# The per-token bonus factor of units 14 to 23: from TensorE products to GpSimd multiplies and a VectorE sum

## The chip, the cores and the metric

One core of one Trainium2 chip runs the whole kernel. The metric is the device time of one execution in microseconds, the median of several runs; lower is better.

## The reference

Two stages follow one another. The first is a linear attention with decay over 4 batches, 8 heads, 768 tokens and 48 channels per head; the second routes each of the 3072 resulting rows to one of 8 experts.

```python
# attention, for each token t, per batch and head
cur = u*k_t (outer) v_t
y_t = r_t @ (state + cur)
state = w * state + k_t (outer) v_t
# experts, x = y as (3072, 384)
logits = x @ w_gate + modality_bias[modality_id];  e_idx = argmax(logits)
out[mask e] = gate_w[mask e] * (relu(x[mask e] @ w1[e]) @ w2[e])
```

The part of `r_t @ cur` is what the change touches. It equals `d * v_t`, where `d = sum over the 48 channels of r*u*k` is one number per token and head. In the kernel `d` is a tile of 128 tokens by 8 heads.

## The kernel before, in words

**Units.** The attention is cut into 24 units of 128 tokens, `(b, c)` with the chunk `c` (0 to 5) in the outer loop and the batch `b` (0 to 3) in the inner one. A unit's inputs come in two layouts. `turned` (L297) loads r and k with channels on the partitions, as the tile `ud`; `lines` (L306) loads k and v with a token per partition, as the tile `kv`. The input array `in_pt` holds k, r and v side by side for each token; `lines` reads the first and the third.

**One unit on the engines.** GpSimd makes `rc` (r times powers of the decay, `decay`, L318), `kt` (k times powers, for the state, `carry`, L325) and, in `own_keys` (L330), `rk`, the product of `rc` and `kc`. VectorE makes `kc` (k times powers, `keys`, L337) and multiplies the scores by the causal mask (`causal`, tile `at`, L378). TensorE makes the scores (`psc`, L372), then in `values` the state's part of the output (L400), the part from the scores (L407), for chunks 0 to 4 the state's update (`pst`, L418), and last, in `bonus` (L346), the factor `d` of the next unit: eight matmuls with 64 columns of `rk` as weights and two columns of `uw` (w times u, one column per head of a pair) as the moving operand, in fp32. They write columns 384 to 391 of the PSUM tile `pst` in whose first 384 columns the state's update lies; `pst` has one buffer. `taken` (L351) on VectorE copies those columns to `d`, and `own` (L359) on ScalarE multiplies `v` by `d`, head by head, into `dv`. From unit 11 on (`BARE`) VectorE adds `dv` to the output (`token`, L435). From chunk 3 on VectorE adds `pst` to the state (`state`, L469), after ScalarE has decayed it (`fade`, L388).

**What runs beside it.** From step 11 on the same engines also work for the first expert. The rows of a group of two to four units are scored (`logits`, L508; `choose`, L518 to L549), counted and placed (L558 to L580, `ahead`, L704 to L727) and sent to DRAM by indirect DMAs from GpSimd (`send`, L596). Blocks of 128 sent rows come back by DMA (`s_turn`, tiles `mxT` and `mt`), and TensorE multiplies them by the first expert's weights: `s_up` (`phs`, L963), `s_down` (`pos`, L1037 and L1042), with ScalarE and VectorE between them (`hh`, L967; `hl`, L972). Odd steps 11 to 21 hold an `s_up`, the even steps after them the `s_down`.

**Order.** Up to the loop over the remaining blocks (L1380) the order on each engine is written out by hand, in `run`: each engine takes its instructions strictly in that order. In step `i` GpSimd's order is: `own_keys(i+1)`, sends, `decay(i+3)`, the give-out of a finished block (L931 to L933), `carry(i+2)`. SP issues `turned(i+5)`, `lines(i+4)`, then the transposing DMA of the finished unit `i-1` (`flip`, L490), a sixth of the second expert's weights in steps 15 to 20 (`raw`, L871), and the turns. The tags `rk` and `kc` have two buffers, `rc` four, `kv` five.

Of the kernel before, what the change touches and what calls it, by code (L numbers as in the profile page):

```python
# [9 lines left out]
F32 = mybir.dt.float32  # L10
# [6 lines left out]
AX = mybir.AxisListType  # L17

P = 128
B, H, S, D = 4, 8, 768, 48  # L20
NCH = S // P
NPR = H // 2
NT = B * S
DM = H * D
# [14 lines left out]
NJ = 40  # L39

BARE = 11

FILL = {1: 4, 2: 4, 3: 2, 4: 2, 5: 2}

# [9 lines left out]
class _Kernel:  # L54
# [251 lines left out]
    def lines(self, i):  # L306

        b, c = self.units[i]
        kv = self.a.tile([P, 2 * DM], F32, tag="kv", name=f"kv{i}", bufs=5)
        self.nc.sync.dma_start(kv.rearrange("p (q d) -> p q d", q=2), self.pt[b * NCH + c].rearrange("p (q d) -> p q d", q=3)[:, ::2])  # L310
        self.ctx_[i].update(k=kv[:, :DM], v=kv[:, DM:])

    def decay(self, i, n=1):
        nc, u = self.nc, self.ctx_[i]
        u["rc"] = self.a.tile([P, NPR, P], F32, tag="rc", name=f"rc{i}", bufs=4)
        for q in range(n):
            s = slice(q * NPR // n, (q + 1) * NPR // n)
            nc.gpsimd.tensor_mul(u["rc"][:, s], u["rT"][:, s], self.powr[:, s])  # L318
# [7 lines left out]

    def own_keys(self, i):
        nc, u = self.nc, self.ctx_[i]
        u["rk"] = self.a.tile([P, NPR, P], F32, tag="rk", name=f"rk{i}")
        nc.gpsimd.tensor_mul(u["rk"], u["rc"], u["kc"])  # L330

# [16 lines left out]
    def taken(self, i):  # L348
        u = self.ctx_[i]
        u["d"] = self.a.tile([P, H], F32, tag="d", name=f"d{i}", bufs=4)  # L350
        self.nc.vector.tensor_copy(u["d"], u["pd"])  # L351

    def own(self, i, q):
        nc, u = self.nc, self.ctx_[i]
# [35 lines left out]
    def values(self, i):  # L390
        nc, u = self.nc, self.ctx_[i]
        b, c = self.units[i]
        st = self.st[c % 2]
        py = u["py"] = self.ps_y.tile([P, 512], F32, tag="y", name=f"py{i}")
        if c:
            for pr in range(NPR):
                c0 = pr * 2 * D
                for q in range(2):
                    t = slice(64 * q, 64 * q + 64)
                    nc.tensor.matmul(py[t, c0 : c0 + 2 * D], u["rc"][:112, pr, t], st[:112, b, pr, :], start=pr == 0, stop=False, skip_group_check=True)  # L400

        for h in range(H):
            pr, j = divmod(h, 2)
            sl = slice(h * D, (h + 1) * D)
            for q in range(2):
                t = slice(64 * q, 64 * q + 64)
                nc.tensor.matmul(py[t, sl], u["at"][:, j * NPR + pr, t], u["v"][:, sl], start=c == h == 0, stop=h == H - 1 and i >= BARE, skip_group_check=True)  # L407
        if i + 1 < len(self.units):
            pst = u["pst"] = self.ps_s.tile([P, 512], F32, tag="s", name=f"pst{i}")
        if c < NCH - 1:  # L410
            faded = self.early(c)
            for pr in range(NPR if faded else 0):
                c0 = pr * 2 * D
                nc.tensor.matmul(pst[:112, c0 : c0 + 2 * D], self.dg[:112, pr, :], st[:112, b, pr, :], start=pr == 0, stop=False, skip_group_check=True)
            for h in range(H):
                j = h % 2
                sl = slice(h * D, (h + 1) * D)
                nc.tensor.matmul(pst[64 * j : 64 * j + D, sl], u["kt"][:, h, :], u["v"][:, sl], start=not faded, stop=True, skip_group_check=True)  # L418
        if i + 1 < len(self.units):
            self.bonus(i + 1, pst)  # L420

    def owned(self, i):
        nc, u = self.nc, self.ctx_[i]
        py = u["py"]
        if i < BARE:
            for q in range(2):
# [3 lines left out]
    def token(self, i):  # L430
        nc, a, u = self.nc, self.a, self.ctx_[i]
        b, c = self.units[i]
        u["x"] = u["py"][:, :DM]
        if i >= BARE:
            nc.vector.tensor_add(u["x"], u["x"], u["dv"])  # L435
# [17 lines left out]
    def early(self, c):  # L453

        return 0 < c and c * B + B - 1 <= BARE

# [416 lines left out]
    def norm(self, junk, q):  # L873
        self.nc.scalar.activation(junk, self.raw[:, q * WQ : (q + 1) * WQ], AF.Square, accum_out=self.ssq[:, q : q + 1])
# [175 lines left out]
    def run(self):  # L1050
        nc, tc, m = self.nc, self.tc, self.m
# [25 lines left out]
        def plan(step, f):  # L1077
            at.setdefault(step, []).append(f)

        def piece(e, q):  # L1080
            if q == 0:
                self.eid = nc.sync.value_load(self.ctl[:, e : e + 1], min_val=0, max_val=E - 1)
            self.load(self.eid, NQ, q)

        def scales(key, half):
            for _ in self.scales_(key, slice(half, half + 1), self.ps_a, "big"):
                pass
# [13 lines left out]
        plan(3, lambda: fills.append(self.setup4()))  # L1101
        plan(4, lambda: fill(99))
        plan(6, self.setup5)
        O = 2
        first, second = (lambda q: lambda: piece(0, q)), (lambda q: lambda: piece(1, q))
        norm = lambda q: lambda: self.norm(junk, q)
        split = lambda q: lambda: self.split(q)
        for q in range(NQ):
            plan(O + (q + 1) // 2, first(q))
            plan(O + 2 + (q + 1) // 2, norm(q))  # L1110
            plan(15 + q, second(q))
            plan(17 + q, norm(q))
        plan(O + 4, lambda: scales("w1", 0))
        plan(O + 6, lambda: (scales("w2", 1), self.undo()))
        for q, i in enumerate((7, 7, 8, 9, 9, 10)):
# [11 lines left out]
        def each(i, *fs):  # L1127
            for f in fs:
                if live(i):
                    f(i)  # L1130


        def fill(n=1):
            while n and fills:
                g = fills.pop(0)
                if next(g, fills) is not fills:
                    fills.append(g)
                    n -= 1

        for i in range(NU - 1):  # L1140
# [12 lines left out]
            if down is not None:  # L1153
                self.s_high(down, 1)
                self.s_down(down, 0)
            first = i <= BARE
            each(i, self.taken) if i and first else None
# [52 lines left out]
            for p in range(2):  # L1210
                for h in range(2):
                    c, r = divmod(i + 1 - 2 * p - h, B)
# [16 lines left out]
        i, j = NU - 2, NU - 1  # L1229
# [208 lines left out]
```

## Time and profile before

| what | value |
|---|---|
| median of 3 runs | 374.55 us (373.67 to 376.98) |
| the profiled execution's own time | 376.96 us |
| its span | 375.2 us |
| TensorE busy over the span | 340.5 us (91%) |
| VectorE, ScalarE, GpSimd busy | 231.2, 176.7, 165.3 us |
| mean granted TensorE clock | 0.958 |

The profile shows one execution. Its rows of time give the start of a group of instructions, how long the group took, the engine, the line of the kernel, the operation and its tiles, how many instructions there are, and in square brackets how long the engine had been idle before and what ended that. The rows of stretches give for each engine the busy time with the number of instructions, then the granted TensorE clock, the busy share of the DMA engines and the GB/s moved. An fp32 matmul shows as two instructions.

### The profile page before, as it was taken

To read this page: it belongs to the slowest core of one execution; us is meant where nothing else is said; L and a number is where in the kernel's file an instruction comes from. 1 tells how busy PE (TensorE), PEld (TensorE's weight loads), DVE (VectorE), ACT (ScalarE), POOL (GpSimd) and SP (SyncE) were. 2 spreads that over 40 slices of the span, in tenths; PEclk is the share of its full clock that TensorE was granted. 3 is DMA by queue.
4 is the path that set the end of the run, shared out by engine and by line. 5 is a ranking of instruction groups with operands and counts; after the bars stand their busy time and mean duration, and the time that the engine had idled before them with its cause. 6 is when DMAs were issued, how large, how long until landed. Compare 5 with 4: busy or idle time off the path is not lost. (4 is left out here: it accounts for less than half of the span.)

```text
span 375.2 us, 14969 instructions
## 1 busy us (share of the span) xinstructions
PE 340.5 (91%) x5432; PEld 271.4 (72%) x5432; DVE 231.2 (62%) x741; ACT 176.7 (47%) x474; POOL 165.3 (44%) x243
## 2 busy tenths in 40 slices
PE   8976968878999999899999999599899999999883
PEld 3654857766879788687888777387687778887661
DVE  6986737788689969858945863028733322224960
ACT  6557646746646645755764222027222222256720
POOL 7996444395358468554425431014421111202731
PEclk9997869898899999999999999699999999999999
DMA  7997999875779499993546254211752122111110
GB/s 160 257 200 163 271 221 228 160 191 128 142 157 189 114 221 250 210 248 114 166 69 107 86 151 172 63 42 42 271 136 60 42 52 53 42 42 42 42 54 4
DMA packets 61166, 50.31 MB, mean 134 GB/s; under 512 B 47288, under 2 KB 54727, under 8 KB 60864
## 3 DMA queue, kind: packets, MB, share of 16 engines
q1 hardware_dynamic: 57920, 40.21, 50.4%
q0 software_dynamic: 3200, 9.47, 6.9%
q8 instruction: 31, 0.51, 0.6%
q14 instruction: 15, 0.12, 0.1%
HBM read 28.39 MB, written 11.83 MB: 107 GB/s over the span
## 5 line engine op out<-in xcount | busy, mean ns | idle before, releaser
L963 PEld LDWEIGHTS <-whi 128*128 128x128 f16 x1248 | 74.6, 100 | 4.6 <-issue 2.0
L1037 PEld LDWEIGHTS <-hh 128*128 128x128 f16 x416 | 38.9, 98 | 29.8 <-issue 4.2
L359 ACT ACTIVATE dv<-kv,d 128x48 f32<-128x48 f32 x192 | 48.1, 325 | 4.5 <-DVE d L351 4.4
L330 POOL TENSOR_TENSOR rk<-rc,kc 128x512 f32<-128x512 f32 x24 | 30.6, 1274 | 43.9 <-DVE kc L337 16.9
L963 PE MATMUL phb<-mxT,whi 128*128 128x128 f16 x720 | 48.8, 222 | 0.0
L963 PEld LDWEIGHTS <-wlo 128*128 128x128 f16 x624 | 38.0, 98 | 1.5 <-DVE wlo L909 1.5
L318 POOL TENSOR_TENSOR rc<-ud,powr 128x512 f32<-128x512 f32 (+1 forms) x27 | 32.3, 1202 | 12.8 <-PE py L400 7.9
L972 DVE SCALAR_TENSOR_TENSOR hl<-phb,hh 128x256 f16<-128x256 f32 (+1 forms) x45 | 22.7, 512 | 22.4 <-ACT hh L967 18.5
L967 ACT ACTIVATE hh<-phb 128x256 f16<-128x256 f32 (+1 forms) x45 | 20.2, 453 | 34.2 <-PE L963 12.5
L378 DVE TENSOR_TENSOR at<-psc,mask 128x512 f32<-128x512 f32 x48 | 32.3, 683 | 3.4 <-PE psc L372 3.0
L596 POOL DMA_INDIRECT rows<-row,posi x24 | 24.4, 1018 | 21.4 <-issue 15.1
L1042 PEld LDWEIGHTS <-hl 128*128 128x128 f16 x208 | 19.5, 99 | 19.8 <-issue 4.4
L963 PE MATMUL phs<-mxT,whi 128*128 128x128 f16 x480 | 31.4, 224 | 0.0
L372 PE MATMUL psc<-rc,kc 48*64 48x128 f32 x768 | 29.9, 294 | 1.7 <-issue 1.4
L1047 DVE TENSOR_SCALAR fac<-mt,wf 128x1 f32<-128x1 f32 x16 | 3.4, 212 | 44.6 <-ACT otb L923 39.4
L923 ACT ACTIVATE otb<-po,fac 128x384 f32<-128x384 f32 x15 | 8.6, 576 | 47.0 <-PE phb L963 37.1
L1042 PE MATMUL po<-whi,hl 128*128 128x384 f16 x128 | 25.0, 338 | 5.4 <-DVE mt L1337 4.0
L1037 PE MATMUL po<-wlo,hh 128*128 128x384 f16 x128 | 26.3, 326 | 3.0 <-DVE wlo L909 3.0
L407 PE MATMUL py<-kv,at 128*64 128x48 f32 x768 | 27.5, 225 | 1.7 <-DVE row0f L680 1.1
L963 PE MATMUL phb<-mxT,wlo 128*128 128x128 f16 x360 | 27.9, 219 | 1.2 <-DVE wlo L909 1.2
L407 PEld LDWEIGHTS py<-kv,at 128*64 128x64 f32 x768 | 26.5, 142 | 3.2 <-DVE row0f L680 1.8
L909 DVE SCALAR_TENSOR_TENSOR wlo<-raw,ws,whi 128x1024 f16<-128x1024 f32 (+1 forms) x18 | 24.8, 1417 | 5.3 <-ACT whi L904 5.3
(259 smaller groups left out, 654.3 us busy)
## 6 DMA issues: line engine op xcount, KB each, us to landing
ud<-in_pd SPq DMA_DIRECT2D x48, 192.0 KB, 5.0
kv<-in_pt SPq DMA_DIRECT2D x24, 384.0 KB, 5.6
raw<-in_w SPq DMA_DIRECT2D x12, 512.0 KB, 5.6
raw<-in_w SPq DMA_DIRECT2D x2, 1536.0 KB, 6.8
rows<-pad SPq DMA_DIRECT2D x10, 193.0 KB, 2.6
rows<-row,posi POOLq DMA_INDIRECT x24, 4.6
xT<-row SPq DMA_TRANSPOSE x23, 4.2
xn<-rows SPq DMA_TRANSPOSE x16, 3.2
```

Of the source, the lines that this page charges most:

```text
L318: nc.gpsimd.tensor_mul(u["rc"][:, s], u["rT"][:, s], self.powr[:, s])
L330: nc.gpsimd.tensor_mul(u["rk"], u["rc"], u["kc"])
L359: nc.scalar.activation(u["dv"][:, sl], u["v"][:, sl], AF.Copy, scale=u["d"][:, h : h + 1])
L372: nc.tensor.matmul(u["ps"][j][s, pr * P : (pr + 1) * P], u["kc"][r, pr, s], u["rc"][r, pr, :], start=True, stop=True)
L378: nc.vector.tensor_mul(u["at"][:, j * NPR : (j + 1) * NPR, :], u["ps"][j].rearrange("p (q t) -> p q t", q=NPR), self.mask.unsqueeze(1).to_ ...
L407: nc.tensor.matmul(py[t, sl], u["at"][:, j * NPR + pr, t], u["v"][:, sl], start=c == h == 0, stop=h == H - 1 and i >= BARE, skip_group_che ...
L596: i = nc.gpsimd.indirect_dma_start(out=self.rows, out_offset=bass.IndirectOffsetOnAxis(ap=u["posi"][:, b : b + 1], axis=0), in_=u["row"][: ...
L909: self.nc.vector.scalar_tensor_tensor(self.wlo[:, sl], self.raw[:, sl], sc, self.whi[:, sl], ALU.mult, ALU.subtract)
L963: self.nc.tensor.matmul(ph[:, q * P : (q + 1) * P], w[:, c0 : c0 + P], self.xT[:, xq, t * P : (t + 1) * P], start=i == q == 0, stop=i == l ...
L972: self.nc.vector.scalar_tensor_tensor(self.hl[:, f0 : f0 + fb, r], p3, 0.0, self.hh[:, f0 : f0 + fb, r], ALU.max, ALU.subtract)
L1037: self.nc.tensor.matmul(po[:, :DM], self.hh[:, f, t * P : (t + 1) * P], w[:, c0 : c0 + DM], start=n == q == f == 0, stop=False)
L1042: self.nc.tensor.matmul(po[:, :DM], self.hl[:, f, t * P : (t + 1) * P], self.whi[:, c0 : c0 + DM], start=False, stop=f == FB - 1)
```

## The change

A new constant `LATE` is 14. For units 14 to 23:

- `lines` also loads r with a token per partition (tile `r`, four buffers, 128 by 384 fp32), right behind the load of `kv` on SP's queue;
- `own_keys` multiplies r by k and the result by u, two GpSimd instructions of 128 by 384 each, in place of the one of 128 by 512 that made `rk`. The result `ru` takes the buffers of tag `rk`;
- `taken` sums `ru` over the 48 channels of each head on VectorE, in place of the copy out of PSUM;
- `bonus` is not issued, and units 20 to 23, which have no state update, no longer take a `pst` tile.

In step 9 a new `wide_u` loads u, repeated on all 128 partitions, as the tile `ub`.

```diff
+LATE = 14
...
         self.ctx_[i].update(k=kv[:, :DM], v=kv[:, DM:])
+        if i >= LATE:
+            r = self.ctx_[i]["r"] = self.a.tile([P, DM], F32, tag="r", name=f"r{i}", bufs=4)
+            self.nc.sync.dma_start(r, self.pt[b * NCH + c][:, DM : 2 * DM])
+
+    def wide_u(self):
+
+        self.ub = self.c.tile([P, DM], F32, name="ub")
+        self.nc.sync.dma_start(self.ub, self.u.to_broadcast([P, DM]))
...
     def own_keys(self, i):
         nc, u = self.nc, self.ctx_[i]
+        if i >= LATE:
+            t = u["ru"] = self.a.tile([P, NPR * P], F32, tag="rk", name=f"ru{i}")[:, :DM]
+            nc.gpsimd.tensor_mul(t, u["r"], u["k"])
+            nc.gpsimd.tensor_mul(t, t, self.ub)
+            return
...
-        self.nc.vector.tensor_copy(u["d"], u["pd"])
+        if i >= LATE:
+            self.nc.vector.reduce_sum(u["d"], u["ru"].rearrange("p (h d) -> p h d", h=H), axis=AX.X)
+        else:
+            self.nc.vector.tensor_copy(u["d"], u["pd"])
...
-        if i + 1 < len(self.units):
+        if i + 1 < LATE or c < NCH - 1:
             pst = u["pst"] = self.ps_s.tile([P, 512], F32, tag="s", name=f"pst{i}")
...
-        if i + 1 < len(self.units):
+        if i + 1 < LATE:
             self.bonus(i + 1, pst)
...
+        plan(9, self.wide_u)
```

On TensorE, in `values` of unit 14 (`py` is the unit's output, `pst` its state update, `pos` and `hl` belong to the expert's block), before:

```order
L400 MATMUL py_2299<-st_94,rc_1709 64x96 x8
L407 MATMUL py_2299<-kv_1503,at_2080 64x48 x16
L418 MATMUL pst_2324<-kv_1503,kt_91 48x48 x8
L346 MATMUL pst_2324<-uw,rk_2230 64x2 x8
L1042 LDWEIGHTS hl
L1042 MATMUL pos_2233<-whi,hl 128x384
```

and now, with the line numbers of the changed kernel:

```order
L418 MATMUL py_2305<-st_94,rc_1715 64x96 x8
L425 MATMUL py_2305<-kv_1505,at_2091 64x48 x16
L436 MATMUL pst_2330<-kv_1505,kt_91 48x48 x8
L1060 LDWEIGHTS hl
L1060 MATMUL pos_2239<-whi,hl 128x384
```

The eight products for `d` are gone from between the state's update and the next block's product; nothing else has moved. The same holds in the units 13 to 22.

On GpSimd, around the steps 14 and 15, before:

```order
L318 TENSOR_TENSOR rc_2263<-ud_86,powr 128x512
L325 TENSOR_TENSOR kt_89<-kv_1825,wtok 128x384
L330 TENSOR_TENSOR rk_2384<-rc_2055,kc_2266 128x512
L318 TENSOR_TENSOR rc_2435<-ud_87,powr 128x512
L931 TENSOR_TENSOR puts_2438<-ids,none 128x1
```

and now:

```order
L328 TENSOR_TENSOR rc_2269<-ud_86,powr 128x512
L335 TENSOR_TENSOR kt_89<-kv_1831,wtok 128x384
L341 TENSOR_TENSOR ru_2384<-r_1833,kv_1831 128x384
L342 TENSOR_TENSOR ru_2384<-ru_2384,ub 128x384
L328 TENSOR_TENSOR rc_2436<-ud_87,powr 128x512
L949 TENSOR_TENSOR puts_2439<-ids,none 128x1
```

Two multiplies stand where one stood, and they read `r`, `kv` and `ub`, no longer `kc`, which VectorE makes. On VectorE the sum stands where the copy stood, between the same neighbours:

```order
L536 TENSOR_SCALAR xinv_1391<-sx_1390 128x4
L367 TENSOR_REDUCE d_2259<-ru_2009 128x8
L487 TENSOR_TENSOR st_93<-st_93,pst_2127 48x4x48
L539 TENSOR_REDUCE L_2262<-pr_2175 128x32
L487 TENSOR_TENSOR st_93<-st_93,pst_2127 48x4x48
```

Before, the second of these rows was the copy:

```order
L518 TENSOR_SCALAR xinv_1391<-sx_1390 128x4
L351 COPY d_2253<-pst_2116 128x8
L469 TENSOR_TENSOR st_93<-st_93,pst_2116 48x4x48
L521 TENSOR_REDUCE L_2256<-pr_2172 128x32
L469 TENSOR_TENSOR st_93<-st_93,pst_2116 48x4x48
```

Only the operation and its source differ: `ru` in SBUF for `pst` in PSUM.

## The prediction

> **What bounds the kernel now.** I read the busy time by stretch first, cut where the products for `d` that the change removes begin and end, and where the attention's tail ends (columns: length, then TensorE, its weight loads, VectorE, ScalarE, GpSimd busy with counts, granted clock, DMA share, GB/s).
>
> ```profile
> 117.50:191.00 73.50, 72.14 (x1511) 60.92 (x1506) 59.43 (x181) 44.01 (x140) 39.65 (x53) 1.00 0.82 180
> 191.00:235.70 44.70, 44.22 (x587) 34.60 (x585) 26.40 (x140) 13.87 (x33) 16.50 (x42) 1.00 0.47 122
> 235.70:239.70 4.00, 0.01 (x1) 0.04 (x2) 0.46 (x2) 0.00 (x0) 0.00 (x0) 0.80 0.29 49
> ```
>
> In the first stretch TensorE is busy 72.14 of 73.5 us and has no idle that another engine causes: its one stall there, of 1.36 us, is in the next fence. VectorE is busy 59.43 us and leaves 14.07. So TensorE's instruction stream sets the pace, and what is taken out of it moves all that follows. Then I read TensorE's order of time around one of these products (in unit 14's `values`, for unit 15's `d`) and the total of L346 in the stretch.
>
> ```profile
> 126.13 0.53 PE L418 MATMUL pst<-kv,kt 128*48 128x48 f32 x16
> 126.49 0.60 PE L346 MATMUL pst<-uw,rk 112*64 112x2 f32 x16
> 127.02 1.47 PE L1042 MATMUL pos<-whi,hl 128*128 128x384 f16 x8
> 154.40 0.88 PE L372 MATMUL psc<-rc,kc 48*64 48x128 f32 x23 [1.36 <-issue]
> 117.50:191.00 73.50, 5.97 (x160) 5.52 (x160) 1.00 0.82 180
> ```
>
> The last row is L346 alone: 160 instructions, ten units of 16. Not all of the 5.97 us is path, because matmuls overlap: from the start of L346 at 126.49 to the start of the next group at 127.02 it is 0.53 us.
>
> **The change part by part.** *Removed from TensorE:* 10 x 0.53 = 5.3 us, all of it in a stream without gaps, at a granted clock of 1.00. This is the one large term.
>
> *GpSimd:* one multiply of 128x512 becomes two of 128x384.
>
> ```profile
> 117.06 1.04 POOL L325 TENSOR_TENSOR kt<-kv,wtok 128x384 f32<-128x384 f32 x1
> 118.01 1.30 POOL L330 TENSOR_TENSOR rk<-rc,kc 128x512 f32<-128x512 f32 x1
> 119.24 1.30 POOL L318 TENSOR_TENSOR rc<-ud,powr 128x512 f32<-128x512 f32 x1
> 120.47 1.02 POOL L325 TENSOR_TENSOR kt<-kv,wtok 128x384 f32<-128x384 f32 x1
> 124.32 1.28 POOL L330 TENSOR_TENSOR rk<-rc,kc 128x512 f32<-128x512 f32 x1 [2.83 <-DVE ebx L284]
> L330 POOL TENSOR_TENSOR rk<-rc,kc 128x512 f32<-128x512 f32 x10 | 12.8, 1282 | 20.1 <-DVE posi L578 14.4 <-DVE ebx L284 5.7
> L325 POOL TENSOR_TENSOR kt<-kv,wtok 128x384 f32<-128x384 f32 x6 | 6.1, 1019 | 0.0
> ```
>
> `kt` has the new shape, 1.02 us; so 2 x 1.02 - 1.28 = 0.76 us more per unit, 7.6 in all, on an engine that is idle for 73.5 - 39.65 = 33.9 us of the stretch. The row at 120.47 makes the `kt` of unit 16, which TensorE takes two steps later, and `rc` is three units ahead, so 0.76 us is hidden there. What changes more is when it works. Before the `rk` at 124.32 GpSimd idled for 2.83 us until VectorE's `kc` was there (20.1 us ahead of ten `rk`). `ru` needs only `r`, `kv` and `ub`, loaded steps before: GpSimd will run on from `kt` into the two multiplies at once, and no longer leaves VectorE a pause in which to make `kc`.
>
> *VectorE:* the copy becomes a sum, and its small operations meet GpSimd elsewhere.
>
> ```profile
> L351 DVE COPY d<-pst 128x8 f32<-128x8 f32 x12 | 1.9, 157 | 2.5 <-PE pst L346 2.4
> 215.76 0.28 DVE L754 TENSOR_REDUCE en<-pk 128x16 f32<-128x128 f32 x1
> 118.73 2.80 DVE L518 TENSOR_SCALAR xinv<-sx 128x4 int32<-128x4 int32 x1
> 122.69 0.69 DVE L972 SCALAR_TENSOR_TENSOR hl<-phs,hh 128x512 f16<-128x512 f32 x1
> 124.37 0.19 DVE L528 TENSOR_REDUCE mx<-L 128x4 f32<-128x32 f32 x1
> L337 DVE TENSOR_TENSOR kc<-ud,powk x25: 425/684/1823, 6.2 to 178.4; 128x512 f32<-128x512 f32 x23, 128x256 f32<-128x256 f32 x2
> ```
>
> No row has a sum of 384 elements. From 0.19 us for 32 and 0.28 for 128, 0.94 ns per element gives an estimate of 0.52 us; against the copy's 0.16 that is 0.36 more per unit, 3.6 in all. The bounds: 0.12 more (the 0.28 of the 128-element sum) and 1.1 (if a sum is held up by one multiply of 1.02 us as well). I take 0.36: the sum at 124.37 took 0.19 us while `rk` ran from 124.32 to 125.60, so sums are not held up. Other VectorE work is: `xinv`, on 4 elements, took 2.80 us and ended at 121.53, just after `kt` ended at 121.49; and one `kc` took 1823 ns for a median of 684.
>
> How much of this reaches TensorE is read from the distance between a VectorE result and its use. The `hl` that ends at 123.38 is used at 127.02: 3.6 us. The closest pair I found is in steps 16 and 17, where the group's placing also stands:
>
> ```profile
> 142.62 1.91 DVE L723 SCALAR_TENSOR_TENSOR ctl<-done,fur 1x1 int32<-1x1 f32 x1
> 146.19 0.71 DVE L469 TENSOR_TENSOR st<-st,pst 48x192 f32<-48x192 f32 x2
> 148.91 0.53 PE L418 MATMUL pst<-kv,kt 128*48 128x48 f32 x16
> ```
>
> The state's sum ends at 146.90 and frees the only `pst` buffer, which L418 takes at 148.91: 2.0 us. TensorE now comes 0.53 us sooner from the same point, two sums add 0.72, so 0.8 us is left, against perhaps 0.8 more of blocking (0.5 for a placing operation and 0.3 for `kc`, each behind part of a 1.02 us multiply) and less at L723, whose 1.91 us ended with a multiply too. It may just miss there. I book 0.3 us; bounds 0 (all hidden) and 2.6 (both steps late by 1.3). The `d` of the last units comes earlier, since it no longer waits for TensorE, but ScalarE's `dv` is not what TensorE waits for: nothing.
>
> *DMA and SP:* 11 loads of 192 KB more.
>
> ```profile
> ud<-in_pd SPq DMA_DIRECT2D x48, 192.0 KB, 5.0
> 135.00:150.00 15.00, 15.00 (x322) 12.57 (x320) 12.76 (x42) 7.83 (x28) 9.85 (x15) 1.00 1.11 242
> 150.00:165.00 15.00, 13.64 (x266) 11.09 (x263) 12.70 (x36) 10.77 (x34) 7.38 (x10) 1.00 1.18 226
> 51.80 0.78 PE L508 MATMUL pr<-wghl,xT 128*128 128x16 f16 x23 [3.32 <-issue]
> ```
>
> A load of this size lands in 5.0 us and is wanted three steps later, and its buffer is free when it is issued, so on SP it costs only its issue; the flip and the weights' pieces behind it come that much later, with steps to spare. But from 135 to 165 the DMA engines are full, and there about four of these loads come on top. TensorE's stalls "for nothing that the profile shows" fall in such full stretches: 1.36 us at 154.40, 3.32 at 51.80. I take zero, because the program moves only a little against the transfers; bounds -1.36 (the one in the stretch goes) and +3.32 (a second like the longest).
>
> *Sum:* -5.3 + 0.3 = -5.0 us. On the profiled execution: 376.96 - 5.0 = 371.96. Its time lies 2.4 us above the median of the runs, 374.55; on that, **369.55 us**.
>
> **The rivals.** *1. VectorE comes late at the dense places.* `kc` reads two tiles of SBUF, and now meets GpSimd at work in each unit. If it waits for one multiply, 0.36 + 1.02 = 1.38 us per step, 2.76 over steps 16 and 17 against a distance of 2.0 - 0.53 = 1.5: 1.3 us lost, and as much again around steps 18 and 19: 374.55 - 5.3 + 2.6 = 371.85. For it: `xinv` waited 2.80 us through more than one multiply. Against: the second multiply must wait for the first, a break in which VectorE can get in, and other distances are over 3 us. The Trainium skill says so too ("SBUF — State Buffer", Who interferes with whom): VectorE with two SBUF inputs and a GpSimd instruction that reads SBUF exclude each other for the whole instruction, while sums never do on this chip. The rows of `xinv`, `kc` and the sum at 124.37 agree.
>
> *2. VectorE becomes the bound, and the kernel slower.* The place is the whole stretch, the price a wait at `kc` in each unit. It has 14.07 us to spare at the old length; sums take 3.6, so from (14.07 - 3.6) / 10 = 1.05 us of blocking per unit, about one multiply, the stretch is longer than before. At one and a half (1.53 us): 3.6 + 15.3 - 14.07 = +4.8, so 379.4 us. For it: `kc` took 1823 ns once, 1.14 over its median. Against: the 59.43 us already hold blocked time (2.80, 1.91), which moves rather than adds.
>
> *3. One more stall of TensorE's own kind* in the full stretch, by the rows at 154.40 and 51.80 some 1.4 to 3.3 us, say 2.3: 371.85 us again, by another cause.
>
> *4. The gain is absorbed* in the 4 us gap at 235.7.
>
> ```profile
> 207.48 0.22 PE L558 MATMUL pr<-oh,warm 128*128 128x8 f16 x3
> 210.18 0.17 DVE L578 CAST posi<-pos 128x3 int32<-128x3 f32 x1
> 210.62 0.97 POOL L596 DMA_INDIRECT rows<-row,posi  x1 [4.68 <-DVE fur L704]
> SPq L950 <- DMA rows<-row,posi: 4.6, 2, 3.6
> 224.89 9.07 SPq L860 DMA_DIRECT2D rows<-pad  x8
> 235.97 1.26 SPq L950 DMA_TRANSPOSE xn<-rows  x1
> 239.69 2.72 PE L1042 MATMUL po<-whi,hl 128*128 128x384 f16 x8 [4.01 <-DVE mt L1337]
> ```
>
> TensorE waits there for a block that comes through SP: eight pads in a row (9.07 us), then the transposing load. If that chain did not start sooner, the gap would be 9 us and the time 374.55. Against: it begins with sends that wait for positions (210.18), counted by TensorE at 207.48, so it moves with TensorE.
>
> **How the numbers follow.** The forecast 0.52, rival 1 0.18, rival 3 0.15, rival 2 0.08, rival 4 0.07. One per cent, about what a measurement of this kernel can tell from no change, is 3.75 us: faster means below 370.8. Of the forecast 0.49 lies there and 0.03 above; of rivals 1 and 3 0.06 and 0.05; so faster 0.60. Slower, above 378.3, is most of rival 2: 0.06. Same 0.34. The range begins where the saving is whole and the 1.36 us stall goes as well, 374.55 - 5.3 - 1.36 = 367.9, and ends at 373.4: rival 3's upper end, 374.55 - 5.0 + 3.3 = 372.85, and half a microsecond for what rivals 1 and 3 may do together; rivals 2 and 4 lie outside.
>
> **What would show it.** Right: no two-column products after unit 13's; TensorE busy within 1.5 us of the length of the stretch, which is 68 to 69 us from the end of unit 13's state update to the last `d`; sums of 0.4 to 0.6 us; GpSimd's pair right behind `kt`; the gap near 235 still 4 us and 5 us sooner. Wrong: TensorE waiting for `kc`, `st` or `hl` in this stretch, with `kc` over 1 us (rivals 1, 2); new stalls on nothing shown (3); a gap over 6 us (4); or a group after L418 that starts less than 0.5 us sooner than before.

## The result, and the profile after

| kernel | median of its runs | ratio to before, 95% interval |
|---|---|---|
| before (4 runs) | 374.11 us (373.35 to 376.98) | |
| the change (4 runs) | 369.93 us (368.79 to 376.74) | 0.987 (0.982 to 0.992) |

The forecast was 369.55 us, 5.0 below before. By the medians the change took off 4.2 us, by the ratio 4.9. The profiled execution of the change took 370.29 us, with a span of 368.6 us. Some executions of a kernel fall into a slower state, and the ratios here and below leave them out; in the second set of experiments one very low run of the kernel before (368.4 us) puts most of its others into that state, so there I compare the medians of all runs.

The two profiles cannot simply be subtracted: the state's update of unit 13, up to which both kernels give TensorE the same work, begins at 117.17 us before and at 113.31 us after. In nine more profiles of kernels that differ little or not at all ahead of it, it begins between 111.8 and 118.3 us. So I measure from that update's start to the start of the last unit's `values`, which is the same pair of places in every kernel. The stretch before, then of the change (length; TensorE, weight loads, VectorE, ScalarE, GpSimd busy with counts; clock, DMA share, GB/s):

```profile
117.17:194.54 77.37, 76.01 (x1574) 64.17 (x1570) 61.84 (x195) 47.19 (x151) 40.32 (x54) 1.00 0.81 174
```

```profile
113.31:186.39 73.08, 72.07 (x1413) 59.48 (x1409) 64.01 (x194) 46.16 (x150) 46.37 (x63) 1.00 0.89 203
```

TensorE still sets the pace: it is idle for 1.01 us of 73.08. It lost some 160 instructions and 3.94 us of busy time. VectorE gained 2.17 us and GpSimd 6.05. The place around unit 14's state update, and every idle time of TensorE from there to the expert's loop:

```profile
121.84 0.53 PE L436 MATMUL pst<-kv,kt 128*48 128x48 f32 x16
122.30 1.48 PE L1060 MATMUL pos<-whi,hl 128*128 128x384 f16 x8
...
145.50 0.38 PE L981 MATMUL phs<-mxT,whi 128*128 128x128 f16 x4 [0.41 <-issue]
165.85 0.34 PE L1055 MATMUL pos<-wlo,hh 128*128 128x384 f16 x1 [0.55 <-issue]
200.59 0.50 PE L1055 MATMUL pos<-whi,hh 128*128 128x384 f16 x2 [0.26 <-ACT hh L985]
232.47 2.72 PE L1060 MATMUL po<-whi,hl 128*128 128x384 f16 x8 [4.92 <-DVE mt L1356]
```

Before, 0.36 us lay between the start of the state's update and that of the products, and 0.53 between these and `pos`: 0.89 together. Now `pos` follows the update after 0.46. That is **0.43 us saved per unit, not 0.53**. With `L346` gone, the next group does not take its place 0.36 us after the update; it begins 0.10 later. In units 20 to 22, which have no state update, the next group begins 1.02 us after the start of L425 where it was 1.44 after L407: 0.42.

No row in the stretch has TensorE waiting for `kc`, `st` or `hl`. On GpSimd the pair stands right behind `kt`, as forecast:

```profile
116.78 1.01 POOL L335 TENSOR_TENSOR kt<-kv,wtok 128x384 f32<-128x384 f32 x1
117.73 1.00 POOL L341 TENSOR_TENSOR ru<-r,kv 128x384 f32<-128x384 f32 x1
118.82 1.40 POOL L342 TENSOR_TENSOR ru<-ru,ub 128x384 f32<-128x384 f32 x1
121.18 1.28 POOL L328 TENSOR_TENSOR rc<-ud,powr 128x512 f32<-128x512 f32 x1 [0.97 <-PE py L418]
```

Between the pair's two starts lie 1.09 us where the instruction took 1.00, a break of 0.09. `kt` and the first multiply, which do not depend on each other, start 0.95 us apart at 1.01 us of duration: no break. So I put the break down to the second multiply reading what the first wrote. Here VectorE's `kc` began its work in it (118.7 us), and the second multiply took 1.40 us instead of 1.00. On VectorE, the sums, `kc` in the late stretch, and the dense place of steps 16 and 17:

```profile
L367 DVE TENSOR_REDUCE d<-ru x10: 539/542/544, 114.5 to 181.7; 128x8 f32<-128x384 f32 x10
```

```profile
L352 DVE TENSOR_TENSOR kc<-ud,powk x8: 659/680/693, 118.7 to 171.9; 128x512 f32<-128x512 f32 x8
```

```profile
140.97 0.54 DVE L367 TENSOR_REDUCE d<-ru 128x8 f32<-128x384 f32 x1
141.43 0.70 DVE L487 TENSOR_TENSOR st<-st,pst 48x192 f32<-48x192 f32 x2
```

```profile
143.34 0.53 PE L436 MATMUL pst<-kv,kt 128*48 128x48 f32 x16
```

A sum takes 542 ns (minimum, median and maximum lie within 5), so none was held up. No `kc` was, either. The state's sum ends at 142.13 and TensorE takes the buffer at 143.34: 1.2 us left, of 2.0 before.

### The profile page after: what moved, and what is told of

Read it like the earlier page. It is cut to its first block, busy times and chain, and to the rows that moved or that the text cites. A ratio compares the mean times of both kernels' runs of the same rounds, so it can differ in the third digit from the quotient of the medians.

```text
span 368.6 us, 14681 instructions
## 1 busy us (share of the span) xinstructions
PE 335.1 (91%) x5272; PEld 265.7 (72%) x5272; DVE 232.0 (63%) x741; ACT 176.4 (48%) x474; POOL 173.2 (47%) x253
## 5 line engine op out<-in xcount | busy, mean ns | idle before, releaser
L981 PEld LDWEIGHTS <-whi 128*128 128x128 f16 x1248 | 73.5, 99 | 5.2 <-issue 2.2
L981 PE MATMUL phs<-mxT,whi 128*128 128x128 f16 x480 | 30.4, 219 | 0.5 <-issue 0.4
L425 PEld LDWEIGHTS py<-kv,at 128*64 128x64 f32 x768 | 26.8, 144 | 3.5 <-DVE row0f L698 2.2
L425 PE MATMUL py<-kv,at 128*64 128x48 f32 x768 | 27.8, 227 | 1.6 <-DVE row0f L698 1.6
L950 POOL TENSOR_TENSOR seenb<-otb,putb 128x1 int32<-128x1 int32 x15 | 3.8, 254 | 50.3 <-ACT otb L941 47.5
```

The lines of the kernel that those rows point to most:

```text
L981: self.nc.tensor.matmul(ph[:, q * P : (q + 1) * P], w[:, c0 : c0 + P], self.xT[:, xq, t * P : (t + 1) * P], start=i == q == 0, stop=i == l ...
```

## The experiments

Three sets, each on a chip of its own with its own runs of the kernel before (medians 374.23, 374.75 and 386.39 us).

**The change once more** (first set, unaltered).

> The changed kernel once more, unaltered, to have its time beside the other three on one chip, and a second profile of it. Its fast times so far are 368.8 to 370.3 us against 373.4 to 374.6 before, 4.3 us less. Theory: TensorE's stream is shorter by 0.43 us in each of ten units (in the profiles the state's update is followed by the next group after 0.46 us where it was 0.89 us), 4.3 in all, and nothing else moves the time: 369.7 us again. In the profile of the change the gap in TensorE's work near 227 us had grown from 4.0 to 4.9 us. If that is scatter of the pads' transfers, this second profile may have 4 us again; if the change causes it, it is 4.9 again.

Measured: 369.16 us, 0.987 (0.981 to 0.993). The result repeats. The gap near 227 us was 4.63 us, between the two; it is taken up below.

**The products back, all else kept.**

```diff
+        by = u["rk"] if i < LATE else u["rc"]
...
-        if i + 1 < LATE:
+        if i + 1 < len(self.units):
             self.bonus(i + 1, pst)
```

> The changed kernel, with TensorE's products issued again in units 13 to 22, out of the tile rc in place of rk, and read by no one; d still comes from r. So GpSimd's pair, VectorE's sum and the loads of r stay, and only TensorE's saving is gone. Theory (TensorE's stream is the whole gain, the rest is hidden): 0.43 us in each of ten units come back, 4.3 us over the change, 373.9 us, no different from before. The prediction's own price, 0.53 us a unit: 5.3 over the change, 374.9. Rival (part of the gain comes from GpSimd, which no longer waits for kc): less than 3 us over the change, under 372.7. Rival (the added work costs something that the saving covers): over 375, slower than before.

Measured: 374.58 us, 1.002 (0.998 to 1.006): no different from before. So within that uncertainty the whole gain is TensorE's, and the added work (10 loads, 20 multiplies for 10, 10 sums for 10 copies) costs nothing that can be measured: 0.6 us, give or take 1.4. Rows of this kernel show the old distances, 0.36 and 0.53:

```profile
113.39 0.53 PE L437 MATMUL pst<-kv,kt 128*48 128x48 f32 x16
113.75 0.60 PE L362 MATMUL pst<-uw,rc 112*64 112x2 f32 x16
114.28 1.51 PE L982 MATMUL phs<-mxT,whi 128*128 128x128 f16 x24
...
151.34 0.89 PE L391 MATMUL psc<-rc,kc 48*64 48x128 f32 x24 [2.17 <-issue]
164.93 0.34 PE L437 MATMUL pst<-kv,kt 128*48 128x48 f32 x6 [0.93 <-issue]
```

```profile
113.39:192.65 79.26, 76.16 (x1574) 64.08 (x1570) 63.22 (x194) 46.58 (x150) 45.89 (x63) 1.00 0.86 189
```

TensorE's busy time in the stretch is that of before, 76.16 against 76.01 us, and 3.10 us are stalls for nothing that the profile shows.

**The products gone, nothing added** (the kernel before; d of units 14 to 23 is zero, so that the term d times v is left out there).

```diff
-        self.nc.vector.tensor_copy(u["d"], u["pd"])
+        self.nc.vector.tensor_copy(u["d"], u["pd"] if i < LATE else self.zero[:, :H])
...
+        if i + 1 < LATE:
             self.bonus(i + 1, pst)
```

> The kernel before, with TensorE's products of units 13 to 22 left out and d of units 14 to 23 copied from a tile of zeros, so that the term d times v is missing in those units. No r is loaded, GpSimd still makes rk, VectorE still copies: the saving without any of the added work. Theory (the added work is all hidden): the same time as the change, 369.7 us within 0.7. Rival (part of the full 5.3 us is eaten by the sums, GpSimd or the loads): about 368.7 us, 1 us below the change, with 0.53 us a unit gone from TensorE's stream instead of 0.43.

Measured: 370.88 us, 0.988 (0.982 to 0.994). The change, which has all of the added work, had 0.987 on the same chip, and its median was even 1.7 us lower. A cost of the added work shows in neither run; the two bound it to about 2 us, and not to nothing.

**No loads of r** (v stands in for r, so d is another number in units 14 to 23).

```diff
-            r = self.ctx_[i]["r"] = self.a.tile([P, DM], F32, tag="r", name=f"r{i}", bufs=4)
-            self.nc.sync.dma_start(r, self.pt[b * NCH + c][:, DM : 2 * DM])
+            self.ctx_[i]["r"] = self.ctx_[i]["v"]
```

> The changed kernel without the loads of r of 192 KB: GpSimd multiplies v, k and u instead of r, k and u, so d is another number in units 14 to 23; engine work is the same. Theory (the loads cost nothing): 369.7 us, as the change, within 0.7. Rival (the loads crowd full DMA engines and cost the stalls of 0.41 and 0.55 us at 145 and 165 us, and the 0.9 us by which the gap near 227 us grew): 368 us.

Measured: 369.34 us, 0.985 (0.979 to 0.991), beside 0.987 (0.981 to 0.993) for the change: the medians are 0.2 us apart, and the ratios cannot be told apart. Its profile has no stall in the stretch, and so shows the stream bare:

```profile
116.08:187.52 71.44, 71.44 (x1414) 59.22 (x1410) 63.41 (x194) 45.99 (x150) 46.26 (x63) 1.00 0.84 184
```

TensorE is busy for all of 71.44 us. Against the 76.01 of before, ten products were worth 4.57 us, 0.46 each. That is the upper end: in the other three profiles without products (the change twice, and the kernel before with nothing added) TensorE is busy 71.5 to 72.2 us, which gives 3.8 to 4.5. And 0.3 of the 4.57 lies in one step of before: from unit 17's update to unit 18's it is 10.64 us (148.91 to 159.55), of which 1.36 are the stall, and the 9.28 left are 0.3 longer than the like step from unit 13 to 14 (8.96). Here both steps take 8.53. Without that, the stretch too gives **4.3 us, 0.43 each**. It does not follow that the loads cause the stalls: TensorE's idle time in the stretch was 1.36 us before (no r), 3.10 with products and loads, 1.01 and 0.84 in the two profiles of the change, and 1.78 in the run without either.

**Two more multiplies per unit on GpSimd** (second set; d is r times k times u to the third power in units 14 to 23).

```diff
-            nc.gpsimd.tensor_mul(t, t, self.ub)
+            for _ in range(3):
+                nc.gpsimd.tensor_mul(t, t, self.ub)
```

> The changed kernel with two more multiplies by u on GpSimd in each of the units 14 to 23, one behind the other (d is r times k times u to the third power there, another number): 2.0 us more per unit, 20 in all, GpSimd busy about 64 of 68.5 us in the stretch where it is busy 44. Theory (GpSimd and VectorE only meet now and then, and TensorE waits for neither): 1 to 2 us more than the change where sends and multiplies crowd one step, about 370.7. Rival 2 of the prediction (each multiply on GpSimd keeps VectorE off for as long): VectorE has 13.3 us left, 20 blocked, so 6.7 us more, 375.9.

Measured: 371.06 us, 3.7 below before by the medians; by the ratio 0.990 (0.983 to 0.996). From the unit-13 update (114.76 us) to the last `values` (190.20) it is 75.44 us, 2.4 longer than in the first profile of the change and 3.1 longer than in the second. So by these profiles 20 us more of GpSimd cost 2 to 3 us, somewhat over what I expected, and not 6.7; the unaltered change did not run on this chip. VectorE, which has no more to do than in the change, is busy 70.51 us of this stretch instead of 64.01: the further 6.5 us are time in which its instructions were held up (one `kc` took 1.56 us for 0.68), and most of it did not reach TensorE. The row of this stretch and TensorE's waits in it follow; the waits are small, and the first is at the place that the prediction named:

```profile
114.76:190.20 75.44, 72.18 (x1414) 59.49 (x1410) 70.51 (x194) 45.86 (x150) 66.74 (x81) 1.00 0.90 194
145.55 0.56 PE L437 MATMUL pst<-kv,kt 128*48 128x48 f32 x16 [0.59 <-DVE st L488]
178.18 1.50 PE L982 MATMUL phs<-mxT,whi 128*128 128x128 f16 x24 [0.71 <-ACT ots L942]
182.03 1.30 PE L1056 MATMUL pos<-whi,hh 128*128 128x384 f16 x6 [0.64 <-DVE hl L991]
```

**The sum three times over.**

```diff
-            self.nc.vector.reduce_sum(u["d"], u["ru"].rearrange("p (h d) -> p h d", h=H), axis=AX.X)
+            for _ in range(3):
+                self.nc.vector.reduce_sum(u["d"], u["ru"].rearrange("p (h d) -> p h d", h=H), axis=AX.X)
```

> The changed kernel with VectorE's sum done three times over in units 14 to 23: 2 x 0.54 = 1.08 us more per unit, 10.8 in all, of the 13.3 us that VectorE has left in the stretch. Theory (distance, not busy time, decides: in steps 16 and 17 the state's sum now ends 1.2 us ahead of its use): 2 x 1.08 - 1.2 = 1.0 us lost there, perhaps as much again near steps 18 and 19: 370.2 to 371.2. Rival (VectorE's order is far from the path everywhere): 369.2, nothing lost. Rival (VectorE is next to the bound): 4 us or more lost, 373.

Measured: 379.89 us, 5.1 above before by the medians; by the ratio 1.012 (1.005 to 1.019). My expectation was some 9 us too low, and the rival of VectorE next to the bound was right. The stretch is 79.69 us (118.28 to 197.97), 6.6 longer than the change's. TensorE's waits, and VectorE (the third busy number) by pieces:

```profile
151.06 0.56 PE L437 MATMUL pst<-kv,kt 128*48 128x48 f32 x16 [2.19 <-DVE st L488]
162.49 1.10 PE L391 MATMUL psc<-rc,kc 48*64 48x128 f32 x30 [0.30 <-DVE at L397]
186.02 0.40 PE L391 MATMUL psc<-rc,kc 48*64 48x128 f32 x2 [1.54 <-DVE at L397]
188.54 2.08 PE L1056 MATMUL pos<-whi,hh 128*128 128x384 f16 x6 [0.66 <-DVE hl L991]
```

```profile
141.00:155.00 14.00, 11.81 (x280) 10.60 (x280) 13.35 (x42) 7.25 (x23) 10.96 (x17) 1.00 1.05 276
183.00:195.00 12.00, 9.43 (x127) 6.46 (x125) 11.35 (x31) 8.56 (x27) 3.16 (x5) 0.86 0.38 102
```

VectorE is busy 95% of both pieces, and TensorE, which was full in the change, is not. The change itself already has such a piece, around its steps 20 to 22; the kernel before had 12.85 us there:

```profile
166.00:180.00 14.00, 14.00 (x273) 11.68 (x272) 13.62 (x51) 9.62 (x30) 7.94 (x14) 1.00 0.66 183
```

```profile
173.00:187.00 14.00, 14.00 (x301) 12.13 (x299) 12.85 (x48) 9.31 (x30) 8.18 (x15) 1.00 0.49 141
```

VectorE has 0.38 us of 14 left there. The 9 us that the whole stretch leaves it lie in other steps, where they are of no use. By the medians this kernel is 5.1 us above before, where the change is 3.6 to 5.1 below: 9 to 10 us, of which the stretch holds 6.6. Where the rest lies is not shown.

**LATE at 11**, with u loaded in step 6.

```diff
-LATE = 14
+LATE = 11
...
-        plan(9, self.wide_u)
+        plan(6, self.wide_u)
```

> The changed kernel with LATE at 11 instead of 14 (u is loaded in step 6 instead of 9): three more units take d from r. The changed kernel had 369.16 us (median of six) beside the runs before. Theory (each unit is worth TensorE's 0.43 us wherever the stream has no gap, and the steps 10 to 12 have none): 3 x 0.43 = 1.3 us less, 367.9. Rival (the prediction's 0.53): 367.6, not to be told apart here. Rival (the sooner TensorE waits for ScalarE's dv, as it does once near 91 us for 0.8 to 2.1 us): 369.2, nothing gained.

Measured: median 373.43 us, 1.3 below before by the medians, 0.997 (0.993 to 1.000) by the ratio, where the theory had 6 below. Its profile, the fastest of its runs (368.57 us, 4.9 below its median), does show the saving: the state updates of units 12 and 13 begin 6.65 us apart (106.18 and 112.83), against 7.08 before (110.09 and 117.17).

**LATE at 4**, with u loaded in step 1.

```diff
+LATE = 4
...
+        plan(1, self.wide_u)
```

> The changed kernel with LATE at 4 (u is loaded in step 1): ten more units, 4 to 13, in a part where TensorE already waits for ScalarE (dv and state, 0.8 to 2.1 us each) and for r's powers, and where the DMA engines are full from 40 to 80 us. Theory (TensorE's stream): 10 x 0.43 = 4.3 us less than the change, 364.9. Rival (ScalarE's dv and the state's copy take back what TensorE gives): about 2 us less, 367.2. Rival (loads): ten more loads of 192 KB in full DMA engines cost a stall or two of 1.5 us each: 368 us or more.

Measured: median 372.62 us, 2.1 below before, 1.001 (0.994 to 1.007) by the ratio: the ten further units bring nothing, and seem to lose part of the first ten's gain (the unaltered change is missing in this set, but the change with two more multiplies was 3.7 us below before). The profiled execution took 376.56 us, 3.9 over this kernel's median, so it shows what can happen there, and not what the median is made of. It has one wait that I had not written down, rival 1 of the prediction in another place:

```profile
81.45 0.55 DVE L367 TENSOR_REDUCE d<-ru 128x8 f32<-128x384 f32 x1
81.92 3.00 DVE L352 TENSOR_TENSOR kc<-ud,powk 128x512 f32<-128x512 f32 x1
```

```profile
82.41 1.01 POOL L335 TENSOR_TENSOR kt<-kv,wtok 128x384 f32<-128x384 f32 x1
83.36 1.00 POOL L341 TENSOR_TENSOR ru<-r,kv 128x384 f32<-128x384 f32 x1
84.44 1.34 POOL L342 TENSOR_TENSOR ru<-ru,ub 128x384 f32<-128x384 f32 x1
```

```profile
73.81 1.61 PE L390 MATMUL psc<-rc,kc 48*64 48x128 f32 x32 [1.62 <-DVE kc L352]
85.06 1.10 PE L390 MATMUL psc<-rc,kc 48*64 48x128 f32 x32 [2.60 <-DVE kc L352]
```

`kc` took 3.00 us for 0.68: it stood through the end of a send (until 82.39), `kt` and the first multiply, which do not depend on each other and follow without a break, and finished at 84.92, as the second multiply was stretched to 1.34. TensorE waited 2.60 us for it, six times what a product saves. With the 1.62 us that makes 4.2 us of waiting for `kc`, where the profile of the change has 0.3, at its very start; but a wait of 3.7 us for the load of `xT`, at 53.17, stands in this execution too. That `kc` is what takes back the gain is therefore likely, and not shown. The sum itself took 0.55 in the middle of this.

**LATE at 11 again, u in step 8** (third set, beside the unaltered change).

```diff
+LATE = 11
...
+        plan(8, self.wide_u)
```

> LATE at 11 once more, with u loaded in step 8 instead of 6, beside the unaltered change. With u in step 6 the median of twelve was 373.4 us, beside 374.8 for the kernel before, where three more units should have given 368; but its own profile shows 0.43 us saved in each of the units 11 to 13. Theory (TensorE's stream; the surplus of the first run was scatter of that chip): 1.3 us below the unaltered change. Rival (the load of u in step 6 stands ahead of loads that are waited for in the full DMA engines): with u in step 8 1.3 us below as well, and then the first result was the load's. Rival (VectorE, busy 11.7 of 13.3 us there, is late in steps 10 to 13): at or above the unaltered change again.

Measured: 384.09 us, 0.994 (0.990 to 0.997), against 382.79, 0.991 (0.988 to 0.994), for the change. Again nothing gained, and 1.3 us above the change by the medians, so the load of u in step 6 was not to blame; that is what the rival of a late VectorE forecast. One new wait stands in its profile (0.62 us for `kc` at 90.17), which is too little to settle it: where the 1.3 us of units 11 to 13 go stays open.

**The change beside it**, and **LATE at 19.**

> The changed kernel, unaltered, beside the next three on one chip, since times of one kernel differ by some microseconds from chip to chip and run to run. Theory: 1.3% below the kernel before, as in both measurements so far (0.987 and 0.987), that is 369 to 370 us.

> The changed kernel with LATE at 19 instead of 14: five units have the change instead of ten. Theory (each unit is worth 0.43 us of TensorE's stream): 5 x 0.43 = 2.15 us over the change, 371.5, halfway to the kernel before. Rival (a part of the gain is one single stall or wait that goes, not a price per unit): the change's own time if it lies in units 19 to 23, or the time before if it lies in units 14 to 18.

Measured: the change 382.79 us, 0.991 (0.988 to 0.994), LATE at 19 382.89 us, 0.992 (0.988 to 0.995). On this chip the change is worth 3.6 us by the medians, and half of its units seem to give all of it. Half of the gain would be 0.9955, just outside the interval of LATE at 19 (it ends at 0.9952); it fits only if the change's own gain is larger than its 0.991 says, which that interval allows. So the times do not exclude the rival that a part of the gain is a single stall. The profile of LATE at 19 shows both distances in one execution, for steps of one kind (units 14 to 15 with products, 18 to 19 without): 7.07 and 6.65 us.

```profile
127.27 0.53 PE L436 MATMUL pst<-kv,kt 128*48 128x48 f32 x16
134.34 0.53 PE L436 MATMUL pst<-kv,kt 128*48 128x48 f32 x16
...
161.96 0.53 PE L436 MATMUL pst<-kv,kt 128*48 128x48 f32 x16
168.61 0.53 PE L436 MATMUL pst<-kv,kt 128*48 128x48 f32 x16
```

So the price per unit is shown in the stream, and how much of it reached this chip's times is not settled. What differs there is seen in the profile of the change on it: TensorE stalls in bursts. In the stretch alone 3.8 us of them fall. One burst of 3.5 us in all lies 10 to 15 us ahead of the gap's place; its two longest stalls:

```profile
216.14 0.27 PE L981 MATMUL phs<-mxT,whi 128*128 128x128 f16 x2 [1.16 <-issue]
217.65 0.27 PE L981 MATMUL phs<-mxT,whi 128*128 128x128 f16 x2 [1.24 <-issue]
```

TensorE then comes to the gap's block later than the block does: there is no gap at all in this profile.

**Pads in two queues.**

```diff
-            r = nc.sync.value_load(self.ctl[:, ENDS + e : ENDS + e + 1], min_val=0, max_val=E * CAP + P)
-            i = nc.sync.dma_start(self.rows[bass.ds(r, P), :], self.pad)
+            q = nc.gpsimd if e in (1, 3, 5) else nc.sync
+            r = q.value_load(self.ctl[:, ENDS + e : ENDS + e + 1], min_val=0, max_val=E * CAP + P)
+            i = q.dma_start(self.rows[bass.ds(r, P), :], self.pad)
```

> The changed kernel with three of the eight pads in a row issued by GpSimd's queue instead of SP's. In the change TensorE's gap near 227 us had grown from 4.0 to 4.6 or 4.9 us, and its chain goes through SP: eight pads one behind the other (8.4 us), then 2.6 to 3.2 us until they have landed, then the block. Theory (the gap is SP's row of pads): five pads take 5.3 us, the block comes 3 us sooner, the gap is 1 to 2 us, and the time 3 us below the unaltered change. Rival (the gap is the landing of the pads' bytes in the DMA engines, whichever queue issues them): less than 1 us.

Measured: 381.70 us, 0.988 (0.983 to 0.994), 1.1 below the change and within the scatter. The trial says nothing of the gap, as this chip had none to close. SP's row of pads did shrink, from 8.65 to 4.83 us, but the block's load came no sooner after it:

```profile
227.28 4.83 SPq L879 DMA_DIRECT2D rows<-pad  x5
237.44 1.26 SPq L969 DMA_TRANSPOSE xn<-rows  x1
```

SP waited 4.3 us there for a table from VectorE (`tab`, L853), which had been hidden behind the pads.

## Why the prediction was right, and which terms were not

*The bound.* Right. TensorE's stream set the pace and still does: 71.44 of 71.44 us busy where no stall falls.

*TensorE's term, 5.3 us.* The mis-sized main term of the sum: it was 4.3 by the distances (0.43 a unit), 4.6 at most by the whole stretch. The step that failed is "from the start of L346 to the start of the next group it is 0.53 us". That is the group's place in the old order. What the removal is worth is the distance from the group ahead of it to the group behind it, before and after: 0.89 less 0.46. The prediction had listed "less than 0.5 us sooner" among the signs of being wrong, and this sign came.

*Blocking at steps 16 and 17, 0.3 us.* Nothing was lost: 1.2 us of distance remain where 0.8 were expected. The place was the right one to fear, since the runs with more GpSimd and with more VectorE work both wait there (0.59 and 2.19 us for `st`). The two errors, 0.7 to 1.0 too much and 0.3 too little, cancel in part, which is luck: 4.3 to 4.6 by the terms, 5.0 forecast, 4.2 and 4.9 measured, and 3.6 on the third chip.

*GpSimd, 0.76 us a unit.* Right: 2.0 us for the pair, hidden. *VectorE, 0.36 us a unit for the sum.* Right: 0.542 us for 0.157. Ten of them add 3.9 us, but VectorE's busy time rose by 2.17 only. Of the 1.7 us between, 0.6 is one `row` (L485, now L503), of which nine instead of ten fall into the stretch; the other 1.1 I take for time held up, which moved and shrank.

*DMA, zero.* Right as far as the runs can tell: 0.2 us between the medians with and without the loads, but each ratio is uncertain by 0.6%, 2 us. The bounds of -1.36 to +3.32 for a stall (and rival 3) were fair: TensorE's idle time was 0 to 3.10 us in six profiles. It was 1.36 and 3.10 with the products, 0 to 1.78 without them; six are too few to tell that from chance.

*The gap at 235.7 (rival 4).* The block came with TensorE, as argued, but not wholly: the gap was 4.92 and 4.63 us for 4.01. Over the profiles it follows SP's wait between the last pad and the block's load, which in the change is 228.81 - 225.65 = 3.16 us:

```profile
217.22 8.43 SPq L878 DMA_DIRECT2D rows<-pad  x8
228.81 1.26 SPq L968 DMA_TRANSPOSE xn<-rows  x1
```

It is 2.84 us in the second profile of the change (gap 4.63), 2.01 before (4.01), 2.29 with the products back (3.84), and also 1.88 with LATE at 11 (3.65), which had the least on TensorE. The runs without loads (3.22 us, gap 5.14), without either (2.58, 4.49) and with two more multiplies (2.69, 4.58) fit in; the sum three times over does not (2.13, 5.04). So the gap goes mostly with the pads' landing. Whether the change lengthens it is not settled: in the first two sets and the two profiles ahead of them, those with products have the gap at 3.84 and 4.01, six without them at 4.49 to 5.14, and only LATE at 11 (3.65) and at 4 (3.37) go against that. Some 1 us of the gain may be lost here. What makes a landing long stays open.

*Rival 2.* It did not come, but its way of counting, by free time over the whole stretch, gave VectorE too much room. With the sum three times over, 1.08 us more a unit in the changed kernel, it gives a stretch 0.3 us longer than before (3.6 + 10.8 - 14.07); the stretch was 2.3 longer (79.69 for 77.37), while VectorE still had 3.6 us of it free (76.12 busy). The added work was sums, not blocking, so the rival's own price was not put to the test. TensorE's longest waits there, 2.19 and 1.54 us, fall into the two pieces where VectorE is 95% busy, so the measure of the room is the fullest 14 us (13.62 busy in the change) and not the stretch's average. The change stands closer to VectorE's bound than the prediction thought.

*Rival 1.* Its mechanism is real and its place was wrong: it is seen in the early units (LATE at 4), where `kc` is wanted at once and cost TensorE 2.60 us in one step. What the prediction held against it, the break ahead of the second multiply, is what ended the wait there too, after two multiplies without one. The Trainium skill ("SBUF — State Buffer", Who interferes with whom) has a VectorE instruction with two SBUF inputs contend with GpSimd's reads under an exclusive lock, and sums never on this chip. This `kc` agrees, with 3.00 us for 0.68, and the sums of 0.54 us agree that they are left out of it; what the row adds is a wait through two GpSimd multiplies in a row, and not one. `xinv`, which the prediction has among the rows that agree, reads one tile only and so is no case of two inputs; it was held all the same, 2.80 us through the rest of `rk`, then `rc` and `kt`, three multiplies that do not depend on each other.

## What to carry to other kernels

Price a group that is taken out of a full stream by the distance between its neighbours, before and after, not by its own start to the next start; here that was 0.43 us against 0.53. Read the room on the engine that takes over in pieces of a step or two, because free time elsewhere does not help: VectorE had 9 us free over 73 and 0.38 over the fullest 14. And an exchange that is free in one part of a program (units 14 to 23) may bring nothing in another (units 4 to 13), where TensorE was seen waiting at once for what the exchange delays.

## What the runs showed of the hardware

- Where two GpSimd multiplies did not depend on each other, VectorE's two-input multiply did not get in between them (once seen, 3.00 us for 0.68), nor did a small operation among three (2.80 us); where the second read the first's result, the break was 0.08 to 0.09 us, and the multiply did get in, at the cost of 0.3 to 0.4 us to the second.
- Stalls of TensorE for nothing that the profile shows differ by execution and by chip: 0 to 3.1 us in the stretch in six profiles (in one of them its 0.84 us of idle time waited for a load instead), 3.8 us on the third chip, and a burst of 3.5 us close ahead of the gap on the chip where the kernel before took 386 us, in a profile in which the gap was gone.
